# First batch in four groups per head pair, two 128-token first blocks, and a kept staging tile: a fused attention and two-layer feed-forward kernel

## The chip, the cores and the metric

The kernel runs on one core of a Trainium2 chip. TensorE (PE) multiplies matrices; VectorE (DVE), ScalarE (ACT) and GpSimd (POOL) do the elementwise work; SyncE (SP) issues most transfers. The metric is the device time of one execution in microseconds, as the median of three runs.

## What is computed

Thresholded attention over 4 batches of 8 heads, 576 positions and 64 features; its output, 2304 tokens of 512 features, goes through two feed-forward layers with 2048 hidden features each, all in 32-bit floats:

```python
scores = (q @ k.T) / sqrt(64)
thresh = max(scores) - tau
scores = where(scores >= thresh, scores, -1e9)
attn = exp(scores - max(scores)); attn /= sum(attn) + 1e-9
x = (attn @ v)                       # to [2304 tokens, 512]
h = x @ w_in;  g = where(h > 0, h, exp(min(h, 0)) - 1);  x = g @ w_out     # layer 0
h = x @ w2_in; g = maximum(0.01 * h, h);                 out = g @ w2_out  # layer 1
```

## The kernel before

**Attention.** Heads are worked in pairs, four pairs a batch. The 576 query rows of a batch are cut into nine units of 64 rows, and the units into groups (`GROUPS`): before, each batch has a group of four units and one of five. `group()` loads one tile `in` (keys and queries) and one tile `v` for each group and pair, and then takes the units two at a time: the score matmuls into `s` (L475), scale and row maximum on DVE (L479), threshold (L485), two passes on ACT (L490, L493), reciprocal (L496), and the scaling of `e` on POOL (L498). The probabilities must then be turned so that keys lie on partitions. There are two ways. In the first group of batch 0 (`gi < GP`) TensorE turns them: five 128x128 transposes for each unit into the accumulator tile `y` (L513), copied to `p` by ACT or DVE (L318, L319). In all other groups DVE turns blocks of 32x32 (L518) into `t`, and sixteen transfers move them to `p` (L568). `values()` multiplies `p` by `v` (L582), and a copy writes the result to `x`.

**Layer 0, first half of its hidden features**, is worked beside the attention in seven blocks of 256 tokens (`BESIDE`). A block has eight steps: `step_h` (four matmuls of 128 features each into `h`), the nonlinearity on ACT, POOL or DVE, and two steps later `step_y` into `y`. The first block (`NATIVE = 1`) multiplies plain 32-bit floats (L621, L674); the others split each operand into a high and a low part and make three passes (L624, L678). The tile `y` is one buffer of two banks, used in turn by all transposes of L513 and by the blocks, in the order in which the program names them. The `h` tile holds two steps, `gh` three. `evac_a` copies a block's `y` to the staging tile `ysa` and sends that to memory.

**The rest** follows when the attention is done: `close_attn` gives back its memory, and 512-token blocks run for what is left of layer 0 and for layer 1.

**The order.** Each engine's instructions are put in order ahead of time by a list scheduler in the program (`Order.run`): every operation carries a due time made from the numbers in `KN`, and a choice of engines. On the chip each engine then works strictly in that order, waiting where an operand is not there.

Of the kernel before, what the change touches and what calls it, by code (L numbers as in the profile page):

```python
# [10 lines left out]
F32 = mybir.dt.float32  # L11
# [19 lines left out]
GROUPS = [(b, u0, u1) for b in range(B) for u0, u1 in ((0, 4), (4, NU))]  # L31
UM = 5
WT = 32 * UM
BESIDE = 7
GP = 1
PT = ()
NG = 5
POOLI = 520
SPI = 720
# [4 lines left out]
NATIVE = 1  # L44
# [8 lines left out]
    pad=18, stay=1957.74, late=1.3, margin=0, look=0.00236881, warm=2, tu=2525.65, lead=19496.6, wv0=975.379,  # L53
    wv1=-2861.01, early=3673.33, boff=26347.2, bdt=5788.03, yoff=6965.78, coff=5895.83, wb=140.292, w2a=-207.297,
    b0=0, b1=0, b2=0, bd0=9322.68, vl=22862.5, tl=13509.4, wp0=137202, wp1=-2346.6, o1=-5700.07, o2=1859.51,
    o3=-792.8, o4=-3200.93, o5=4767.88, o6=-24.0285, mo=-2162.59, ka='P', kl='PA', kh='PA', ko='P', kt='D', kx='A',
    kxl='DP', km='DP', kg='A', kgl='DP', kgl1='D', kd='P', kc='AD', kn='P', kv='AD')
# [205 lines left out]
def attn_moe_kernel(ctx, tc, kqv, tau, w1i, w1o, w2i, w2o, yp, out):  # L263
# [20 lines left out]
    ysx = []  # L284
# [95 lines left out]
    ysx.append(ac.tile([128, KC, TA], F32, name="ysa"))  # L380
# [46 lines left out]
    def group(gi, p, vts, held=None):  # L427
# [24 lines left out]
        by_pe = gi < GP or p in PT  # L452
# [236 lines left out]
    ypdone = {}  # L689

    def block(layer, t0, fs, tb, deps, hps, yrings, evac, vt0, dt, reg=False):
        if reg and t0 < NATIVE * TA:
            xc = [(None, x[:, k, t0:t0 + tb], deps[k]) for k in range(KC)]
        else:
            xc = conv_x(t0, tb, deps, vt0 - dt + (KN["coff"] if reg else 0), reg)
        pend, lasty = [], None
        if isinstance(yrings, Ring):
            gen = yrings.new()
            ybank = [(gen, m % 2, m % 2 == 1) for m in range(KC)]

            def ysl(yg, m):
                return yg()[:, m // 2, m % 2 * TA:(m % 2 + 1) * TA]
# [12 lines left out]
        evac(t0, tb, ybank, ysl, lasty, xc, vt0 + len(fs) * dt)  # L715

    def evac_a(t0, tb, ybank, ysl, last, xc, vt):
        ys = ys_r.new()
        done = []
        if ybank[0][0] is ybank[1][0]:  # L720
            yg = ybank[0][0]
            for j in range(2):
                done.append(op(copy_of("AD", 2 * TA, lambda j=j: ys()[:, 2 * j:2 * j + 2, 0:TA],
                                       lambda j=j: yg()[:, j, :].rearrange("p (a b) -> p a b", a=2)),
# [37 lines left out]
    kept, ready = None, {}  # L762
    for gi, p in order:
# [7 lines left out]
        if gi < GP or p in PT or u == NP * NU:  # L771
# [16 lines left out]

    for i in range(BESIDE):
        need = next(n for t, n in ends if t >= (i + 1) * TA)  # L790
        block(0, i * TA, list(range(FH)), TA, x_deps(i * TA, TA), h_a, ya, evac_a,
              need * TU + KN["boff"] + (KN["b0"], KN["b1"], KN["b2"], 0)[min(i, 3)], KN["bd0"] if i == 0 else KN["bdt"],
              reg=True)
# [5 lines left out]
    end_a = op((HOST, 0, lambda: close_attn()), list(od.ops), [], 0)  # L799
# [16 lines left out]
    rest = [(t0, tb) for t0, tb in ((t, min(TB, NT - t)) for t in range(BESIDE * TA, NT, TB))]  # L816
# [76 lines left out]
```

## Time and profile before

| | |
|---|---|
| median of three runs | 1041.89 us (1040.13 to 1044.59) |
| profiled execution | 1044.41 us, its span 1042.6 us |
| PE busy | 1005.2 us, 96% |
| DVE, ACT, POOL busy | 569.2, 507.0, 392.0 us |
| chain that ended last | PE 90% of the span |

Busy time counts an instruction from its start to its end, and matmuls overlap, so work is better counted by the spacing of starts. An instruction's idle time is put down to what released it. The attention runs to about 400 us; after 402 us TensorE has hardly a gap.

### The profile page before, as it was taken

The page shows a single profiled execution, that of the slowest core. Times are in us where ns is not written, and L with a number is a line of the kernel's source. Part 1 is how long each engine was busy: PE and PEld are TensorE (multiplying, and loading weights), DVE is VectorE, ACT ScalarE, POOL GpSimd, SP SyncE. Part 2 cuts the span into 40 slices and gives each one's busy share as a digit, 9 for nine tenths or more (in the row PEclk, how much of TensorE's full clock was granted, in tenths as well). Part 3 has the DMA queues.
Part 4 walks back from the last instruction along what each step waited for, and adds up shares of the span by engine and source line. Part 5 has one row for each costly group of instructions (what it writes and reads, how often), then busy time and mean ns, then how long its engine had stood idle before and what let it go on. Part 6 is the DMA issues. An engine that isn't in the chain of part 4 may idle for free.

```text
span 1042.6 us, 17014 instructions
## 1 busy us (share of the span) xinstructions
PE 1005.2 (96%) x6228; PEld 795.3 (76%) x6228; DVE 569.2 (55%) x1146; ACT 507.0 (49%) x1009; POOL 392.0 (38%) x542
## 2 busy tenths in 40 slices
PE   6869999999999998999999999999999999999998
PEld 3446676677676776888888889888888888888898
DVE  6888778787887856767786457442211311311121
ACT  6967767677777753555455235432222311322221
POOL 5678977567577752444443013440000000000000
PEclk8999999999999999999999999999999999999999
DMA  6676876766778653353443103320100100000010
GB/s 213 209 216 175 221 195 192 227 188 196 201 209 240 192 150 119 102 182 101 143 141 101 61 21 86 118 61 0 41 1 1 41 1 1 22 19 1 1 41 21
DMA packets 47554, 115.93 MB, mean 111 GB/s; under 512 B 9776, under 2 KB 14384, under 8 KB 47472
## 3 DMA queue, kind: packets, MB, share of 16 engines
q1 hardware_dynamic: 42960, 104.36, 33.4%
q0 software_dynamic: 4512, 10.50, 3.7%
q8 instruction: 49, 0.80, 0.3%
q14 instruction: 33, 0.27, 0.1%
HBM read 67.63 MB, written 9.44 MB: 74 GB/s over the span
## 4 chain that ended last, share of the span: by engine, by line
PE 90%; DVE 3%; DMA 2%; ACT 2%; issue 1%; POOL 0%; SPq 0%; ACTq 0%; DVEq 0%; POOLq 0%
PE y L678 37%; PE h L624 22%; PE hb L624 15%; PE v L582 7%; PE s L475 7%; PE y L674 1%; DMA p<-t 1%; PE h L621 1%; DVE w L346 1%; DMA taut<-in_tau_dram 1%; DVE ss L479 1%; DMA wraw<-in_w1i_dram 1%; PE y L513 0%; DVE xl L307 0%; ACT e L493 0%
## 5 line engine op out<-in xcount | busy, mean ns | idle before, releaser
L307 DVE TENSOR_TENSOR gl<-g,gh 128x512 fp32r<-128x512 f32 (+1 forms) x150 | 101.1, 675 | 284.4 <-ACT g L656 265.0
L678 PE MATMUL y<-gh,woh 128*128 128x512 f32 (+1 forms) x704 | 245.5, 349 | 2.1 <-ACT ysa L318 1.4
L678 PE MATMUL y<-gl,woh 128*128 128x512 f32 (+1 forms) x704 | 242.8, 345 | 0.0
L624 PE MATMUL h<-xh,wih 128*128 128x256 f32 (+1 forms) x448 | 153.1, 342 | 9.2 <-ACT g L639 5.1
L678 PEld LDWEIGHTS y<-gh,woh 128*128 128x128 f32 x704 | 132.5, 188 | 29.1 <-issue 8.8
L624 PE MATMUL h<-xl,wih 128*128 128x256 f32 (+1 forms) x448 | 148.6, 332 | 0.7 <-DVE xl L307 0.6
L678 PEld LDWEIGHTS y<-gl,woh 128*128 128x128 f32 x704 | 132.7, 188 | 16.1
L498 POOL TENSOR_SCALAR e<-e,su 128x576 f32<-128x576 f32 x144 | 113.9, 801 | 32.2 <-DVE su L496 30.9
L678 PE MATMUL y<-gh,w 128*128 128x256 f32 (+1 forms) x384 | 124.9, 325 | 0.0
L490 ACT ACTIVATE ss<-ss,thr 128x576 f32<-128x576 f32 x144 | 104.6, 767 | 34.5 <-DVE thr L485 34.4
L479 DVE TENSOR_SCALAR_CACHE_REDUCE ss<-s,scl 128x576 f32<-128x576 f32 x144 | 113.8, 798 | 10.9 <-PE s L475 10.7
L678 PE MATMUL y<-gh,wol 128*128 128x512 f32 (+1 forms) x320 | 117.7, 368 | 0.0
L518 DVE STREAM_TRANSPOSE t<-e 128x640 f32<-128x640 f32 x128 | 101.2, 823 | 17.9 <-POOL e L498 12.5
L493 ACT ACTIVATE e<-ss,taun 128x577 f32<-128x577 f32 x144 | 110.5, 768 | 0.3
L624 PEld LDWEIGHTS h<-xh,wih 128*128 128x128 f32 x448 | 84.2, 188 | 33.2 <-issue 8.8
L475 PE MATMUL s<-in 64*64 64x288 f32 x1152 | 91.3, 428 | 7.8 <-DVE ss L479 7.8
L624 PE MATMUL hb<-xh,wih 128*128 128x512 f32 (+1 forms) x256 | 94.6, 369 | 0.0
L624 PE MATMUL hb<-xl,wih 128*128 128x512 f32 (+1 forms) x256 | 94.5, 369 | 0.0
L582 PE MATMUL v<-p,v 128*64 128x320 f32 (+1 forms) x640 | 87.1, 417 | 5.3 <-DVE p L319 2.3
L624 PEld LDWEIGHTS h<-xl,wih 128*128 128x128 f32 x448 | 84.3, 188 | 10.0 <-DVE xl L307 1.8
L624 PE MATMUL h<-xh,w 128*128 128x256 f32 (+1 forms) x288 | 89.3, 310 | 0.0
L654 ACT ACTIVATE gh<-h 128x512 fp32r<-128x512 f32 (+1 forms) x40 | 22.2, 555 | 132.4 <-PE h L624 132.4
(207 smaller groups left out, 1591.4 us busy)
## 6 DMA issues: line engine op xcount, KB each, us to landing
p<-t SPq DMA_DIRECT2D x128, 100.0 KB, 2.8
p<-t SPq DMA_DIRECT2D x144, 80.0 KB, 3.3
v<-in_kqv_dram SPq DMA_DIRECT2D x32, 320.0 KB, 3.8
in<-in_kqv_dram SPq DMA_DIRECT2D x16, 608.0 KB, 4.2
in<-in_kqv_dram SPq DMA_DIRECT2D x16, 544.0 KB, 4.0
wraw<-in_w1i_dram SPq DMA_DIRECT2D x16, 512.0 KB, 4.3
wraw<-in_w1o_dram SPq DMA_DIRECT2D x16, 512.0 KB, 3.6
wraw<-in_w2i_dram SPq DMA_DIRECT2D x16, 512.0 KB, 3.5
```

The costliest lines, as they stand in the source:

```text
L307: return pick(who, D=(dve(n), lambda: nc.vector.tensor_tensor(**args()), PORT), P=(pool_tt(n), lambda: nc.gpsimd.tensor_tensor(**args())))
L346: ob = op((DVE, dve(512), lambda: nc.vector.scalar_tensor_tensor(out=b().bitcast(U32), in0=top(), scalar=0x80000000, in1=b().bitcast(U32), ...
L475: nc.tensor.matmul(s[z]()[64 * h:64 * h + 64, i, 0:HALF], q()[r, at:at + 64], k()[r, h], start=True, stop=True)
L479: om = [op((DVE, dve(S) + 160, lambda z=z: nc.vector.tensor_scalar(out=ss[z]()[:, 0:S].rearrange("p (j c) -> p j c", j=2), in0=s[z]()[:, : ...
L490: o = op((ACT, act(S) + 95, lambda z=z: nc.scalar.activation(out=ss[z]()[:, 0:S], in_=ss[z]()[:, 0:S], func=AF.Prelu, bias=thr()[:, z:z + ...
L493: oe.append(op((ACT, act(S) + 190, lambda z=z: nc.scalar.activation(out=e[z]()[:, 0:S + 1], in_=ss[z]()[:, 0:S + 1], func=AF.Exp, bias=tau ...
L498: on = [op(pick(KN["kn"], P=(pool_ts(S) + 90, lambda z=z: nc.gpsimd.tensor_scalar(out=e[z]()[:, 0:S], in0=e[z]()[:, 0:S], scalar1=su()[:, ...
L518: turned.append(op((DVE, dve(SX) + 70, lambda z=z, cols=cols: nc.vector.transpose(out=blocks(tg).rearrange("p d c q -> p c d q")[:, :, :, ...
L582: nc.tensor.matmul(ps()[64 * h:64 * h + 64, 0:64 * n], v()[:, h, c, :], blocks(pg)[:, 2 * h:2 * h + 2, c], start=(c == 0), stop=(c == 4))
L624: nc.tensor.matmul(hp(), w_()[:, cs], x_()[:, 0:tb], start=(k == 0 and z == 0), stop=(k == KC - 1 and z == 2))
L654: o1 = op((ACT, actp(tb), lambda: nc.scalar.activation(out=gh()[:, cs], in_=hp(), func=AF.Prelu, alpha=0.01)), [o], [hg, gh], vt)
L678: nc.tensor.matmul(ysl(yg, m), w_()[:, cs], g_()[:, 0:tb], start=(first and z == 0 and share == 0), stop=(last and z == 2 and end))
```

## The change

Batch 0 is cut into four groups of 2, 2, 2 and 3 units for each pair (`CUTS`); the first three are turned by TensorE (`GP = 3`). The other batches keep their two groups. The first block of 256 tokens becomes two of 128 (`HEADS`), both in plain 32-bit floats (`NATIVE = 2`); six blocks of 256 tokens follow as before. The staging tile `ysa` moves from the attention's memory to memory that is kept, and the operation that closes the attention's memory depends on what was named before the last block's copies out of `y`, not on those copies and their transfer. The numbers in `KN` differ, with the engines allowed to some operations among them (for example the copies from `v` to `x`: DVE alone; the subtraction `gl` beside the attention: POOL alone).

```diff
-GROUPS = [(b, u0, u1) for b in range(B) for u0, u1 in ((0, 4), (4, NU))]
+CUTS = (2,4,6)
+GROUPS = [(b, u0, u1) for b in range(B) for u0, u1 in zip((0, *(CUTS if b == 0 else (4,))), (*(CUTS if b == 0 else (4,)), NU))]
+HEADS = [(0, 128), (128, 128)]
+FIRST = HEADS + [(t, TA) for t in range(256, 1792, TA)]
-BESIDE = 7
-GP = 1
+GP = 3
-NATIVE = 1
+NATIVE = 2
...
-    ysx = []
+    ysx = [const.tile([128, KC, TA], F32, name="ysa")]
...
-    ysx.append(ac.tile([128, KC, TA], F32, name="ysa"))
...
     def evac_a(t0, tb, ybank, ysl, last, xc, vt):
+        since[0] = len(od.ops)
...
-    for i in range(BESIDE):
-        need = next(n for t, n in ends if t >= (i + 1) * TA)
+    for i, (t0, tb) in enumerate(FIRST):
+        need = next(n for t, n in ends if t >= t0 + tb)
...
-    end_a = op((HOST, 0, lambda: close_attn()), list(od.ops), [], 0)
+    end_a = op((HOST, 0, lambda: close_attn()), od.ops[:since[0]], [], 0)
```

How the order moves is seen at three places. First, TensorE near the start. Names: `s` scores, `y<-ident` a turned unit, `v<-p` the values of a group, `h<-x` the first block. Before:

```order
L475 MATMUL s<-in 64x288 x8
L582 MATMUL v<-p_86,v 64x256 x10
L513 MATMUL y<-ident,e_90 128x128 x5
L475 MATMUL s<-in 64x288 x8
L513 MATMUL y<-ident,e_91 128x128 x5
L621 MATMUL h<-x,w_143 128x256
```

And with the change:

```order
L477 MATMUL s<-in 64x288 x8
L515 MATMUL y<-ident,e_93 128x128 x5
L584 MATMUL v<-p_87,v 64x128 x10
L515 MATMUL y<-ident,e_90 128x128 x5
L477 MATMUL s<-in 64x288 x8
L515 MATMUL y<-ident,e_91 128x128 x5
L623 MATMUL h<-x,w_143 128x128
L584 MATMUL v<-p_86,v 64x128 x10
```

The values of a group now come after every second turned unit, not every fourth, and are half as wide.

Second, TensorE where the first block's `y` begins. Before, it stands behind the sixteenth turned unit and some steps of `h`:

```order
L513 MATMUL y<-ident,e_93 128x128 x5
L582 MATMUL v<-p_87,v 64x256 x10
L621 MATMUL h<-x,w_143 128x256
L621 MATMUL h<-x,w_230 128x256
L475 MATMUL s<-in 64x288 x8
L621 MATMUL h<-x,w_230 128x256 x3
L475 MATMUL s<-in 64x288 x12
L621 MATMUL h<-x,w_324 128x256 x4
L674 MATMUL y<-gh,w_196 128x256 x4
L621 MATMUL h<-x,w_439 128x256 x2
L582 MATMUL v<-p_86,v 64x320 x10
```

With the change:

```order
L477 MATMUL s<-in 64x288 x8
L515 MATMUL y<-ident,e_93 128x128 x5
L584 MATMUL v<-p_87,v 64x128 x10
L676 MATMUL y<-gh,w_178 128x128 x2
L477 MATMUL s<-in 64x288 x4
L676 MATMUL y<-gh,w_178 128x128 x2
L676 MATMUL y<-gh,w_282 128x128 x4
L676 MATMUL y<-gh,w_384 128x128 x4
L477 MATMUL s<-in 64x288 x8
L623 MATMUL h<-x,w_704 128x128 x4
```

It stands behind the twenty-fourth turned unit and the twelfth group's values, with five steps of `h` already ahead of it.

Third, the end of the attention. On DVE, `xh` and `xl` are the split input of the first 512-token block. Before:

```order
L319 COPY ysa<-y 128x512 x2
L319 COPY x<-v 128x2x5x32
L307 TENSOR_TENSOR xl_5030<-x,xh_5011 128x512
L307 TENSOR_TENSOR xl_5034<-x,xh_5028 128x512
```

With the change:

```order
L322 COPY ysa<-y 128x512
L322 COPY x<-v 128x2x5x32
L317 TENSOR_SCALAR xh_5297<-x 128x512
L317 TENSOR_SCALAR xh_5312<-x 128x512
L310 TENSOR_TENSOR xl_5316<-x,xh_5293 128x512
```

Two of the four high parts now stand on DVE (before, all four on ACT). On TensorE the last group's values are followed by six matmuls of the last 256-token block, which before stood ahead of them.

## Rows read from the trace of the kernel before

**Rows 1.** Stretches of 25 us: busy (instructions) by engine, granted clock, DMA share, GB/s.

```profile
25.00:50.00 25.00, 20.98 (x184) 12.48 (x184) 20.28 (x48) 23.18 (x45) 17.42 (x22) 0.93 0.64 201
50.00:75.00 25.00, 17.64 (x124) 10.29 (x116) 22.88 (x47) 19.55 (x40) 17.82 (x25) 0.93 0.74 221
...
425.00:450.00 25.00, 25.00 (x112) 20.68 (x112) 20.29 (x27) 14.53 (x24) 11.41 (x10) 1.00 0.29 90
```

**Rows 2.** TensorE in order of time: start, length, instruction, [idle before <-releaser].

```profile
14.78 1.18 PE L513 MATMUL y<-ident,e 128*128 128x128 f32 x5 [0.57 <-POOL e L498]
...
37.58 0.77 PE L513 MATMUL y<-ident,e 128*128 128x128 f32 x5
38.28 1.20 PE L475 MATMUL s<-in 64*64 64x288 f32 x16
39.41 0.77 PE L513 MATMUL y<-ident,e 128*128 128x128 f32 x5
...
44.44 2.38 PE L582 MATMUL v<-p,v 128*64 128x256 f32 x20 [0.78 <-ACT p L318]
46.75 0.77 PE L513 MATMUL y<-ident,e 128*128 128x128 f32 x5
...
52.27 0.74 PE L513 MATMUL y<-ident,e 128*128 128x128 f32 x5
54.38 2.38 PE L582 MATMUL v<-p,v 128*64 128x256 f32 x20 [1.38 <-DVE p L319]
...
76.56 4.93 PE L582 MATMUL v<-p,v 128*64 128x320 f32 x20 [2.20 <-DMA p<-t]
81.42 1.20 PE L475 MATMUL s<-in 64*64 64x288 f32 x16
...
86.09 1.89 PE L621 MATMUL h<-x,w 128*128 128x256 f32 x8
87.82 0.59 PE L674 MATMUL y<-gh,w 128*128 128x256 f32 x2
...
92.10 2.91 PE L582 MATMUL v<-p,v 128*64 128x320 f32 x20
...
100.47 1.89 PE L621 MATMUL h<-x,w 128*128 128x256 f32 x8
```

**Rows 3.** One longer stretch, columns as in rows 1.

```profile
100.00:350.00 250.00, 243.49 (x2184) 176.26 (x2184) 198.04 (x494) 184.13 (x409) 182.12 (x294) 1.00 0.74 207
```

**Rows 4.** ACT and DVE groups by shape: count, then busy us and mean ns.

```profile
L338 ACT ACTIVATE w<-wraw,lowb 128x512 uint32<-128x512 uint32 x60 | 45.7, 761 | 27.7 <-POOL wil L308 8.8 <-POOL w L308 8.3 <-POOL wol L308 6.5
...
L346 DVE SCALAR_TENSOR_TENSOR w<-wraw,w 128x512 uint32<-128x512 uint32 x64 | 48.0, 750 | 1.2
...
L647 DVE SCALAR_TENSOR_TENSOR g<-g,h 128x512 f32<-128x512 f32 x20 | 13.7, 686 | 0.6
L647 DVE SCALAR_TENSOR_TENSOR gh<-g,h 128x256 f32<-128x256 f32 x8 | 3.3, 413 | 0.8 <-ACT g L639 0.7
```

**Rows 5.** Transfers from 0 to 75 us: packets and bytes; issues, KB each, us to landing.

```profile
DMA packets 4875, 16.07 MB, mean 214 GB/s; under 512 B 736, under 2 KB 736, under 8 KB 4869
in<-in_kqv_dram SPq DMA_DIRECT2D x4, 608.0 KB, 4.0
...
v<-in_kqv_dram SPq DMA_DIRECT2D x6, 320.0 KB, 3.6
```

**Rows 6.** The end of the attention in order of time, TensorE, DVE and ACT.

```profile
395.94 0.39 PE L678 MATMUL y<-gh,woh 128*128 128x256 f32 x1 [0.78 <-DVE ysa L319]
396.50 3.12 PE L582 MATMUL v<-p,v 128*64 128x320 f32 x20
...
399.66 0.49 DVE L319 COPY x<-v 128x320 f32<-128x320 f32 x1 [2.36 <-PE v L582]
401.39 2.20 ACT L313 ACTIVATE xh<-x 128x512 fp32r<-128x512 f32 x4 [9.63 <-DMA yp_dram<-ysa]
402.07 0.50 PE L624 MATMUL h<-xh,wih 128*128 128x512 f32 x1 [2.46 <-ACT xh L313]
```

More of the change, by code (lines that the diff above doesn't have):

```diff
@@ L30 @@
 NU = S // 64
-GROUPS = [(b, u0, u1) for b in range(B) for u0, u1 in ((0, 4), (4, NU))]
+CUTS = (2,4,6)
+GROUPS = [(b, u0, u1) for b in range(B) for u0, u1 in zip((0, *(CUTS if b == 0 else (4,))), (*(CUTS if b == 0 else (4,)), NU))]
+HEADS = [(0, 128), (128, 128)]
+FIRST = HEADS + [(t, TA) for t in range(256, 1792, TA)]
 UM = 5
 WT = 32 * UM
-BESIDE = 7
-GP = 1
-PT = ()
+GP = 3
+PT = set()
 NG = 5
+LP = 0
 POOLI = 520
-SPI = 720
+SPI = 700
 PM = ()
@@ L52 @@
 KN = dict(
[L53 to L57, printed above, removed]
+    pad=18, stay=8085.79, late=1.3, margin=0, look=0.00236881, warm=2, tu=2269.97, lead=19258.9, wv0=5061.38,
+    wv1=-3081.32, early=3673.33, boff=26347.2, bdt=5825.03, yoff=8020.93, coff=5895.83, wb=406.105, w2a=-207.297,
+    b0=0, b1=0, b2=0, bd0=11622.3, vl=20762.4, tl=16711.4, wp0=185209, wp1=-2003.44, o1=-5700.07, o2=1859.51,
+    o3=-57.8519, o4=1496.36, o5=3550.58, o6=-24.0285, mo=-2162.59, ka='P', kl='A', kh='PA', ko='P', kt='D', kx='AD',
+    kxl='DP', km='DP', kg='A', kgl='P', kgl1='DP', kd='P', kc='AD', kn='P', kv='D')
 PE, ACT, DVE, POOL, SP, HOST = "PE", "ACT", "DVE", "POOL", "SP", "HOST"
@@ L689, in attn_moe_kernel, with block @@
     ypdone = {}
-    def block(layer, t0, fs, tb, deps, hps, yrings, evac, vt0, dt, reg=False):
-        if reg and t0 < NATIVE * TA:
+    since = [0]
+    def block(layer, t0, fs, tb, deps, hps, yrings, evac, vt0, dt, reg=False, whole=False):
+        if whole:
             xc = [(None, x[:, k, t0:t0 + tb], deps[k]) for k in range(KC)]
@@ L762, in attn_moe_kernel @@
     kept, ready = None, {}
+    PT.update(order[len(order) - LP:])
     for gi, p in order:
@@ L787, in x_deps @@
                  if b * S + 64 * u0 < t0 + tb and b * S + 64 * u1 > t0] for k in range(KC)]
-    for i in range(BESIDE):
-        need = next(n for t, n in ends if t >= (i + 1) * TA)
-        block(0, i * TA, list(range(FH)), TA, x_deps(i * TA, TA), h_a, ya, evac_a,
-              need * TU + KN["boff"] + (KN["b0"], KN["b1"], KN["b2"], 0)[min(i, 3)], KN["bd0"] if i == 0 else KN["bdt"],
-              reg=True)
+    for i, (t0, tb) in enumerate(FIRST):
+        need = next(n for t, n in ends if t >= t0 + tb)
+        block(0, t0, list(range(FH)), tb, x_deps(t0, tb), h_a, ya, evac_a,
+              need * TU + KN["boff"] + (KN["b0"], KN["b1"], KN["b2"], 0)[min(i, 3)],
+              KN["bd0"] if i < NATIVE else KN["bdt"], reg=True, whole=i < NATIVE)
         if i == NATIVE - 1:
@@ L814, in dt @@
         return 24 * mm(tb)
-    rest = [(t0, tb) for t0, tb in ((t, min(TB, NT - t)) for t in range(BESIDE * TA, NT, TB))]
+    rest = [(t0, tb) for t0, tb in ((t, min(TB, NT - t)) for t in range(sum(FIRST[-1]), NT, TB))]
     ysb = {}
```

10 lines of the change are left out of this document (5 added, 5 removed).

## The prediction

> **What bounds the kernel now.** I read the stretches of 25 us first. From 425 us on TensorE is busy all 25 of 25 us, and from 100 to 350 us 243.5 of 250 [rows 1, 3]; before that it is not: 21.0 of 25 from 25 to 50 us and 17.6 from 50 to 75 us, at a granted clock of 0.93 [rows 1]. So the end is set by TensorE's work plus the time it loses in the first 80 us or so and at the close of the attention. Who holds it up early is read from the busy shares there: from 25 to 50 us ACT is busy 23.2 of 25 us and DVE 20.3, and from 50 to 75 us DVE 22.9 [rows 1]. TensorE is fed at the pace of these two. The order of time then shows single stalls: 1.38 us before the values at 54.38, which wait for a copy of a turned unit, and 2.20 us before those at 76.56, which wait for the transfers of the turned blocks and then take 4.93 us where the same take 2.91 at 92.10 [rows 2]. The other place is the close of the attention: 0.78 us for a copy out of `y`, and 2.46 us before the first 512-wide matmul, because ACT's split of its input waits for the transfer of the staging tile [rows 6].
>
> **The measure.** TensorE works strictly in its order, so I compare two moments: when the changed kernel has as much TensorE work left as the kernel before has at 81.42 us, where its long stalls end. Durations are spacings of starts [rows 2]: two units of scores 1.13 us (38.28 to 39.41), so 0.565 a unit; one turned unit 0.70 (37.58 to 38.28); values of four units 2.31 (44.44 to 46.75, length 2.38), of five, with the same overlap, 2.91 - 0.07 = 2.84; a native 256-wide matmul 1.73 / 4 = 0.43 (86.09 to 87.82).
>
> Before, ahead of 81.42 us stand, by the program's order, 28 units of scores (15.8), 16 turned units (11.2), four values of four units and one of five (9.2 + 2.8), 14 matmuls of `h` and 4 of `y` (7.8): 46.9 us of work. The warm-up is the same in both and left out.
>
> **Groups of 2, 2, 2 and 3, turned by TensorE.** *Added work.* Eight more units are turned: 8 x 0.70 = 5.6 us. Values of two and three units are not in the trace; one step of 64 columns is worth 2.84 - 2.31 = 0.53, so I take 1.25 and 1.78 us. Above, if a turned unit's 0.70 for five passes of 128 columns (0.14 each, two side by side in the 20 passes) is the nearest, it is 1.4; the far end is no gain over the four units' 2.31, below it is half of that, 1.16. With 1.25, a pair costs 3 x 1.25 + 1.78 - 2.31 - 2.84 = 0.4, and four pairs 1.5 us (range +0.4 to +3.5, far end +14). The four groups of batch 0 that DVE turns keep their sixteen transfers each, smaller ones. Eight more loads of `in` and `v` go on SP's queue; with them and all weights, 12 x 0.426 + 4 x 0.492 + 16 x 0.328 + 16 x 0.524 = 20.7 MB are asked for before TensorE's first `y`, against 16.07 MB in the first 75 us before [rows 5]. Loads of 320 KB land in 3.6 us and of 608 KB in 4.0 [rows 5], so the first load, 416 KB where it was 544, saves 0.2 us at most, and I leave it out.
>
> The Trainium skill, "DMA: Bandwidth & Descriptors", section "Anatomy of one DMA", gives a transfer a fixed part of about 2.0 us that size does not change; the two loads agree with a large fixed part. If instead a load went by its bytes alone, 416 KB would land some 0.9 us sooner than 544 and the forecast would be that much lower.
>
> *What it moves.* All transposes and all block accumulations share the one tile `y`, in program order. So the first `y` of the block now waits for the twenty-fourth turned unit, not the sixteenth, although its `h` could start sooner; three `gh` and two `h` let only five steps of `h` (20 matmuls, 4.4 us) run ahead. Before the first `y`, then: 32 units of scores (18.1), 24 turned (16.8), twelve values (15.0), 20 half-width matmuls (4.4): 54.3 us of work.
>
> *When that is.* Before, the first turned unit stands at 14.78 and the sixteenth at 52.27: 2.50 us a unit [rows 2]. With the change the same stretch holds 16 weights in 24 units against 9 in 16; a tenth of a weight more a unit, at 0.76 us on ACT and two operations of 0.75 on DVE [rows 4], is 0.08 to 0.15 us, and twelve small copies to `x` in place of four add about 0.04. The chain on TensorE gives the same. Copy and hops after a turned unit's 0.7 take about 1.4, as the 2.1 us from the turned unit at 52.27 to the values at 54.38 show [rows 2]; so turned unit and copy 2.1, values 1.25, next turned unit and copy 2.1 with the scores beside it, 5.4 for two units. I take 2.7. The twenty-fourth turned unit then starts at 14.78 + 23 x 2.7 = 76.9; from a last turned unit to its values it is 54.38 - 52.27 = 2.1, and the values take 1.25: first `y` at 80.3 us, 1.1 earlier than 81.42.
>
> **Two first blocks of 128 tokens.** 128 matmuls of half width for 64: at half of 0.43 and a little (0.222), 28.4 for 27.7 us, +0.7. If two passes of 128 columns cost 2 x 0.14 each as in a turned unit, +8.1; below, +0. I keep near the half, as the 256-wide ones go by columns. The work left at the first `y` is thus 5.6 + 1.5 + 0.7 - (54.3 - 46.9) = 0.4 us more than before at 81.42. Behind it each step of 128 tokens offers TensorE 1.8 us while its nonlinearity passes ACT, POOL and DVE, all 71 to 92% busy from 50 to 75 us [rows 1]; I allow 2.5 us of waits in the next 20 us against 1.05 before (81.42 to 100.47 holds 18.0 us of work): +1.5 (0 to 5).
>
> On DVE the step of 256 columns takes 413 ns and that of 512 takes 686 [rows 4]; the line through them leaves 140 ns that width does not change, so sixteen narrow ones cost 16 x 0.277 - 8 x 0.413 = 1.1 us more on DVE, beside other work. The Trainium skill, "VectorE: DVE Perf Modes", section "The TRN2 errata", says the same against this part of the change, that small operations pay a fixed latency each and should be widened; the two rows agree. With cost by columns alone the 1.1 would be 0.
>
> **The staging tile kept.** The split of the input no longer waits for the transfer, but in DVE's order it stands behind the copy of the last values. From the end of those values (396.50 + 3.12 = 399.62): copy 0.5, two high parts and one low part about 1.8, a hop, so the second matmul about 2.55 us later; 0.75 of that is now filled by the six matmuls moved behind the values. Some 1.7 us of idle time remain of 0.78 + 2.46, and the next matmul's short wait goes with it: -1.8 (0 to -3.5). If the split still waits for something of the last block, it is 0.
>
> **The numbers in the table** send subtractions to POOL and copies to DVE. From 100 us on TensorE hides these; its gaps up to 350 us were 6.5 us [rows 3], and I leave it at 0, with 3 us either way.
>
> **Sum:** -1.1 + 0.4 + 1.5 - 1.8 = -1.0. Against the profiled execution's 1044.4 us (span 1042.6) that is 1043.4; it lay 2.5 above the median of 1041.89, so **1040.9** in terms of the median. A measurement of this kernel can tell some 0.5%, 5.2 us, from no change.
>
> **Rivals.** *The early stretch runs better than I charge.* In the order DVE copies nine of the 24 turned units (ACT fifteen) and has turned only three itself by the first `y`, so it is freed of part of its load while it is the fuller engine; all weights are asked for before the first transfers of turned blocks, which came 2.2 us late at 76.56 [rows 2] with weights between them in SP's queue. With 2.50 us a unit and no extra waits the first `y` is at 75.6: -4.7 - 1.5 more, -7.2, **1034.7**. Against it speaks ACT, busy 23.2 of 25 us [rows 1], which copies more than before.
>
> *The turning loop becomes the bound, and the kernel is slower.* On TensorE's queue the values of a group now stand after every second unit and wait for the copy of the unit just turned; behind them stand the next turned unit and the scores, so ACT and DVE are fed late too. Before, the waits there were 0.78 and 1.38 us for four units [rows 2]. One such wait for two units is 0.2 to 0.35 us a unit more, and if ACT and DVE, fed late, do not make it up, a unit takes 3.1 us: first `y` at 89.4, +9.1, **1050**. It decides from about 2.97 us a unit, where +6.2 on the forecast makes the kernel over 0.5% slower.
>
> *Transfers become the bound.* At the mean rate of before, 214 GB/s, 20.7 MB take 97 us: +16, **1057**; it decides below 240 GB/s. Against it, the engines of DMA were busy only 0.74 of the time at 221 GB/s [rows 1], which leaves room to about 300.
>
> *The staging tile does nothing* (the memory is still held by the last values): +1.8, **1042.7**.
>
> **How the numbers follow.** The forecast, with the staging rival, holds 0.45, all of it within 0.5% (its own range 1037 to 1045); the better early stretch 0.35, faster; the turning loop 0.15 and the transfers 0.05, slower. So faster 0.35, same 0.45, slower 0.20. The range goes from 1032, a little under the first rival for the waits of the middle (0 to -3), to 1049, below the loop's 1050, and leaves out less than 2 in 10.
>
> **What would show it.** In the profile of the changed kernel: the first `y` of the native block near 80 us; turned units 2.7 us apart, with what ends the idle time before the values of two units; values of two units near 1.25 us; half-width matmuls near 0.22; the gap before the first 512-wide matmul under 2 us, ended by DVE's low part and no longer by a transfer; more than 240 GB/s in the first 75 us. The prediction is wrong if the first `y` comes before 76 or after 86 us, or if TensorE's gaps from 100 to 395 us change by more than 3 us.

## The result and the profile after

The changed kernel takes **1058.85 us** (median of 4 runs, 1056.17 to 1061.53) where the kernel before took 1043.24 on the same chip (4 runs, 1040.13 to 1044.79): ratio 1.0133, 95% interval 1.0096 to 1.0170. By the ratio it is slower by some 14 us (the two medians differ by 15.6); 1040.9 had been forecast, with a range from 1032 to 1049. Its profiled execution took 1058.3 us (span 1056.5), the one before 1044.4 (span 1042.6), so the two traces differ by the same 13.9 us.

A good place to cut both traces is the first 512-wide matmul, where the attention has closed: 402.07 us before [rows 6], 414.72 after. Behind it TensorE is busy nearly all the time and the two kernels need 640.5 and 641.8 us, so 12.65 of the 13.9 us are lost ahead of it and 1.25 behind it. TensorE alone, in stretches (bounds, length, busy and instructions, granted clock, DMA share, GB/s), first the kernel before, then the changed one:

```profile
0.00:402.07 402.07, 368.98 (x3156) 0.98 0.70 200
0.00:100.00 100.00, 78.92 (x586) 0.91 0.65 203
100.00:402.07 302.07, 290.06 (x2571) 1.00 0.71 199
```

```profile
0.00:414.72 414.72, 380.39 (x3485) 0.98 0.69 199
0.00:100.00 100.00, 79.52 (x774) 0.90 0.69 223
100.00:414.72 314.72, 300.88 (x2715) 1.00 0.69 191
```

Busy time rose by 11.4 us (368.98 to 380.39), and idle time, length less busy, did not fall: 33.1 before, 34.3 after. The forecast had 7.8 us of added work (5.6 + 1.5 + 0.7) and an end 1.0 us earlier, so it needed the idle time to shrink by 8.8, to 24.3. In the first 100 us TensorE does 79 us of work in both kernels; the added work is not done there in the gaps, it pushes other work behind 100 us, where busy time grew by 10.8.

The stretches of rows 1 and 3 in the changed kernel (busy and instructions of TensorE, its weight loads, DVE, ACT and POOL, then granted clock, DMA share, GB/s):

```profile
25.00:50.00 25.00, 19.00 (x209) 13.67 (x198) 18.69 (x47) 19.30 (x37) 12.70 (x18) 0.93 0.76 260
50.00:75.00 25.00, 22.51 (x258) 16.14 (x254) 21.68 (x55) 22.47 (x47) 13.30 (x20) 1.00 0.81 257
...
100.00:350.00 250.00, 239.44 (x2190) 177.74 (x2186) 196.72 (x480) 169.92 (x379) 190.18 (x299) 1.00 0.70 196
```

From 50 to 75 us TensorE is fuller than before (22.5 for 17.6), from 25 to 50 us emptier, and from 100 to 350 us it idles 10.6 us in place of 6.5. TensorE in order of time, as rows 2. First, two of the earliest scores in the kernel before:

```profile
9.20 2.20 PE L475 MATMUL s<-in 64*64 64x288 f32 x16 [2.68 <-DVE ss L479]
12.01 2.20 PE L475 MATMUL s<-in 64*64 64x288 f32 x16 [0.61 <-DVE ss L479]
```

Then the changed kernel:

```profile
9.48 2.20 PE L477 MATMUL s<-in 64*64 64x288 f32 x16 [2.90 <-DMA in<-in_kqv_dram]
12.58 2.20 PE L477 MATMUL s<-in 64*64 64x288 f32 x16 [0.91 <-DMA in<-in_kqv_dram]
16.04 1.33 PE L515 MATMUL y<-ident,e 128*128 128x128 f32 x5 [1.26 <-POOL e L500]
...
34.47 0.76 PE L515 MATMUL y<-ident,e 128*128 128x128 f32 x5
...
39.53 2.30 PE L584 MATMUL v<-p,v 128*64 128x128 f32 x20 [1.30 <-DVE p L322]
41.76 1.33 PE L515 MATMUL y<-ident,e 128*128 128x128 f32 x5
...
64.72 0.77 PE L515 MATMUL y<-ident,e 128*128 128x128 f32 x5
65.41 1.20 PE L477 MATMUL s<-in 64*64 64x288 f32 x16
66.61 0.74 PE L515 MATMUL y<-ident,e 128*128 128x128 f32 x5
68.12 1.31 PE L584 MATMUL v<-p,v 128*64 128x128 f32 x20 [0.78 <-ACT p L321]
69.37 0.77 PE L515 MATMUL y<-ident,e 128*128 128x128 f32 x5
...
81.64 0.77 PE L515 MATMUL y<-ident,e 128*128 128x128 f32 x5
84.05 1.31 PE L584 MATMUL v<-p,v 128*64 128x128 f32 x20 [1.64 <-ACT p L321]
85.29 0.71 PE L676 MATMUL y<-gh,w 128*128 128x128 f32 x4
...
86.58 2.50 PE L676 MATMUL y<-gh,w 128*128 128x128 f32 x20
89.01 1.20 PE L477 MATMUL s<-in 64*64 64x288 f32 x16
...
95.77 0.71 PE L623 MATMUL h<-x,w 128*128 128x128 f32 x4 [1.15 <-DVE gh L649]
```

The turned units stand at 16.04 (first) and 81.64 (twenty-fourth), 2.85 us a unit; the first `y` of the native block at 85.29 (70.99 in the kernel before; the 81.42 us that the prediction measures from is a later moment). A pair of units without other matmuls between can be read from 64.72 to 69.37: turned unit 0.69, scores 1.20, turned unit 0.73, 0.78 of waiting for its copy, values 1.25, together 4.65 us. Other pairs take longer, by matmuls of `h`, by longer waits, and by the clock: the pair from 34.47 to 41.76 takes 7.29, with values that wait 1.30 us and then take 2.23 in place of 1.25. What TensorE waited for from 14 to 85 us (us in all, times, the longest):

```profile
PE v L584 <- ACT p L321: 6.5, 6, 1.6
PE y L515 <- DVE p L322: 2.3, 3, 1.0
PE v L584 <- DVE p L322: 2.2, 2, 1.3
```

These are waits for copies of turned units, 11.0 us of the 13.6 that TensorE idles there; none of its waits there is for a transfer.

The close of the attention, as rows 6, TensorE and then DVE and ACT:

```profile
410.14 2.91 PE L584 MATMUL v<-p,v 128*64 128x320 f32 x20
...
414.72 0.50 PE L626 MATMUL h<-xh,wih 128*128 128x512 f32 x1 [0.77 <-ACT xh L316]
```

```profile
413.10 0.49 DVE L322 COPY x<-v 128x320 f32<-128x320 f32 x1 [2.16 <-PE v L584]
414.04 0.76 DVE L317 TENSOR_SCALAR xh<-x 128x512 fp32r<-128x512 f32 x2 [0.45 <-PE y L680]
414.03 1.16 ACT L316 ACTIVATE xh<-x 128x512 fp32r<-128x512 f32 x2 [6.86 <-PE y L680]
```

TensorE idles 0.77 us before its first 512-wide matmul where 0.78 + 2.46 stood around the last values [rows 6]. ACT's split starts 0.44 us after DVE's copy of the last values, and what released it was no transfer. Transfers from 0 to 75 us, as rows 5:

```profile
DMA packets 5865, 17.91 MB, mean 239 GB/s; under 512 B 672, under 2 KB 672, under 8 KB 5857
```

### The profile page after: what moved, and what is told of

Its sections match the earlier page's. It is cut to its first block, busy times and chain, and to the rows that moved or that the text cites. A ratio compares the mean times of both kernels' runs of the same rounds, so it can differ in the third digit from the quotient of the medians.

```text
span 1056.5 us, 17766 instructions
## 1 busy us (share of the span) xinstructions
PE 1017.1 (96%) x6556; PEld 814.8 (77%) x6556; DVE 581.0 (55%) x1187; ACT 491.3 (47%) x979; POOL 405.7 (38%) x565
## 4 chain that ended last, share of the span: by engine, by line
PE 82%; DVE 6%; DMA 3%; issue 3%; POOL 3%; ACT 2%; SPq 1%; DVEq 0%; POOLq 0%; ACTq 0%
PE y L680 33%; PE h L626 20%; PE hb L626 14%; PE v L584 6%; PE s L477 5%; PE h L623 1%; PE y L676 1%; DMA p<-t 1%; DVE t L520 1%; DVE ss L481 1%; PE y L515 1%; DVE xl L310 1%; DMA in<-in_kqv_dram 1%; DVE w L349 1%; DMA taut<-in_tau_dram 1%
## 5 line engine op out<-in xcount | busy, mean ns | idle before, releaser
L310 DVE TENSOR_TENSOR gl<-g,gh 128x512 fp32r<-128x512 f32 (+1 forms) x122 | 91.3, 748 | 278.2 <-ACT g L658 260.1
L311 POOL TENSOR_TENSOR gl<-g,gh 128x256 fp32r<-128x256 f32 (+1 forms) x54 | 42.4, 788 | 315.9 <-ACT g L658 207.8
L492 ACT ACTIVATE ss<-ss,thr 128x576 f32<-128x576 f32 x144 | 104.6, 767 | 35.3 <-DVE thr L487 34.8
L500 POOL TENSOR_SCALAR e<-e,su 128x576 f32<-128x576 f32 x144 | 107.7, 758 | 20.9 <-DVE su L498 19.0
L520 DVE STREAM_TRANSPOSE t<-e 128x640 f32<-128x640 f32 x120 | 95.2, 825 | 15.2 <-POOL e L500 8.5
L584 PE MATMUL v<-p,v 128*64 128x128 f32 (+3 forms) x800 | 90.0, 372 | 10.6 <-ACT p L321 6.5
```

The costliest lines, as they stand in the source:

```text
L310: return pick(who, D=(dve(n), lambda: nc.vector.tensor_tensor(**args()), PORT), P=(pool_tt(n), lambda: nc.gpsimd.tensor_tensor(**args())))
L311: P=(pool_tt(n), lambda: nc.gpsimd.tensor_tensor(**args())))
L492: o = op((ACT, act(S) + 95, lambda z=z: nc.scalar.activation(out=ss[z]()[:, 0:S], in_=ss[z]()[:, 0:S], func=AF.Prelu, bias=thr()[:, z:z + ...
L500: on = [op(pick(KN["kn"], P=(pool_ts(S) + 90, lambda z=z: nc.gpsimd.tensor_scalar(out=e[z]()[:, 0:S], in0=e[z]()[:, 0:S], scalar1=su()[:, ...
L520: turned.append(op((DVE, dve(SX) + 70, lambda z=z, cols=cols: nc.vector.transpose(out=blocks(tg).rearrange("p d c q -> p c d q")[:, :, :, ...
L584: nc.tensor.matmul(ps()[64 * h:64 * h + 64, 0:64 * n], v()[:, h, c, :], blocks(pg)[:, 2 * h:2 * h + 2, c], start=(c == 0), stop=(c == 4))
```

## The experiments

Theory: the parts of the change add up, and the added work of the groups lies in idle time. Rivals: the table holds the loss; the groups or the narrow blocks cost by themselves. All ratios are against the kernel before, run beside each. The last four columns are read from the profiled execution up to the first 512-wide matmul: its start, TensorE's busy and idle time, and the time that TensorE spent at 1.2 GHz (summed up to 430 us over stretches of 5 us, each counted as length x (1 - granted clock) / 0.5). These columns are of one execution each, and that can lie off the median: by 3.9 us below it in 13 and 3.5 in 14. The last one differs between executions of the same kernel: over the 71 executions of the kernel before that stand beside these runs the granted clock of the whole span went from 0.984 to 0.993, by the same count 34 to 15 us at 1.2 GHz, some 22 in the mean; the profiled one is at 0.992. The changed kernel's four runs are at 0.990 and 0.991, some 21 us, so its loss is not one of the clock.

| kernel | ratio (95%) | start | busy | idle | 1.2 GHz |
|---|---|---|---|---|---|
| before | 1 | 402.1 | 369.0 | 33.1 | 17.1 |
| changed | 1.0133 (1.0096-1.0170) | 414.7 | 380.4 | 34.3 | 20.4 |
| 1 before, staging kept | 0.9986 (0.9968-1.0004) | 401.3 | 369.7 | 31.6 | 17.0 |
| 2 before, changed table | 1.0165 (1.0146-1.0185) | 416.4 | 377.0 | 39.5 | 34.2 |
| 3 changed, groups of before | 1.0144 (1.0120-1.0168) | 416.4 | 375.1 | 41.4 | 20.5 |
| 4 changed, one first block | 1.0127 (1.0101-1.0153) | 413.7 | 378.8 | 34.8 | 13.6 |
| 5 changed, table of before | 1.0091 (1.0059-1.0123) | 412.1 | 380.3 | 31.8 | 17.0 |
| 6 before, groups and staging | 1.0135 (1.0103-1.0168) | 418.8 | 379.8 | 38.9 | 20.5 |
| 7 before, narrow blocks and staging | 1.0101 (1.0064-1.0138) | 412.3 | 375.7 | 36.6 | 27.4 |
| 8 before, table: engines only | 1.0134 (1.0094-1.0174) | 414.4 | 375.1 | 39.3 | 23.8 |
| 9 before, table: numbers only | 1.0109 (1.0065-1.0153) | 411.5 | 373.0 | 38.5 | 20.4 |
| 10 before, `kx` alone | 1.0074 (1.0049-1.0098) | 409.0 | 373.2 | 35.8 | 20.4 |
| 11 before, `tu` + 1% | 0.9977 (0.9955-1.0000) | 399.3 | 369.8 | 29.5 | 17.2 |
| 12 changed, `kx` of before | 1.0107 (1.0076-1.0137) | 411.3 | 377.6 | 33.7 | 13.7 |
| 13 before, longer turned units | 1.0022 (1.0000-1.0045) | 402.5 | 372.2 | 30.3 | 13.7 |
| 14 before, matmuls halved | 1.0013 (0.9989-1.0036) | 400.6 | 370.1 | 30.5 | 17.2 |
| 15 changed, longer turned units | 1.0167 (1.0134-1.0199) | 417.7 | 386.4 | 31.4 | 13.7 |
| 16 changed, less work on ACT | 1.0112 (1.0085-1.0140) | | | | |
| 17 changed, less work on DVE | 1.0122 (1.0097-1.0147) | 415.3 | 381.5 | 33.8 | 20.5 |
| 18 before, staging and `tu` + 1% | 0.9968 (0.9950-0.9986) | 398.0 | 368.7 | 29.4 | 13.7 |

### One part at a time (1 to 7)

```
1, in before:  ysx = [const.tile([128, KC, TA], F32, name="ysa")]
               close_attn() waits for od.ops[:since[0]], not for list(od.ops)
2, in before:  KN = the changed kernel's table
```

> The kernel before with one part of the change: the staging tile kept and the close of the attention no longer behind the last block's copies. Theory (TensorE pays for added work and for the late start, and the staging part gains): TensorE's gaps at the close fall from 0.78 + 2.46 + 0.22 us to about 1.0, the first 512-wide matmul at about 399.7 to 400.5 instead of 402.07, time 1.5 to 2.5 us under before. Rival (the loss sits in the close or in what follows it): no gain or a loss here, and gaps after the close.

> The kernel before with the changed table of numbers alone. Theory (the structure costs, not the table): within 4 us of before. Rival (the table, which hands subtractions to POOL and copies to DVE, makes waits between 100 and 400 us): 5 to 10 us slower than before, with TensorE's gaps from 100 to 350 us well above the 6.5 us of before.

The staging tile alone gives some 1.5 us, which the interval cannot tell from nothing; the trace shows the gap before the first 512-wide matmul at 0.72 us, ended by ACT's split, where 2.46 stood [rows 6], but that matmul came at 401.3 us and not at 399.7 to 400.5. The table alone costs 17 us, where "within 4 us" had been expected: that theory fell. Its 14.4 us ahead of the first 512-wide matmul are 6.4 us of idle time and 8.0 us of busy time with the same matmuls. In this execution the second is mostly the clock: 17 us more at 1.2 GHz, of which some 14 ahead of the close, worth at most 7 us at half speed. Over all runs that share is smaller: the four of kernel 2 are at 0.982 to 0.987, 33 us at 1.2 GHz in the mean, 11 more than the kernel before, worth at most 5.5 of the 17 us. And kernel 9 has 4.0 us more busy time with no more time at 1.2 GHz ahead of its close (3.4 of its 20.4 us lie behind it), so not all such busy time is the clock. The pattern can be read in one place of kernel 2:

```profile
129.21 0.39 PE L624 MATMUL h<-xh,wih 128*128 128x256 f32 x1 [1.58 <-DVE xh L314]
131.93 0.58 PE L624 MATMUL h<-xl,wih 128*128 128x256 f32 x1 [2.33 <-POOL xl L308]
...
134.78 4.10 PE L582 MATMUL v<-p,v 128*64 128x256 f32 x20
```

```profile
130.00:135.00 5.00, 2.60 (x10) 0.65 0.65 172
135.00:140.00 5.00, 5.00 (x37) 0.67 0.94 271
100.00:350.00 250.00, 237.67 (x2089) 0.99 0.71 201
```

Two waits, 3.9 us together, for the halves of an input split that the table now sends to DVE and POOL; behind them, at a granted clock of 0.67, the values of four units take 4.10 us where they take 2.38 [rows 2]. The last line is the longer stretch of rows 3, with gaps of 12.3 us for 6.5.

```
3, in changed:  CUTS = (4,)   GP = 1
4, in changed:  HEADS = [(0, 256)]   NATIVE = 1
5, in changed:  KN = the table of before
6, in before's table:  groups of the change, one first block of 256, staging kept
7, in before's table:  groups of before, two first blocks of 128, staging kept
```

> The changed kernel with batch 0 cut and turned as before (groups of 4 and 5, the first turned by TensorE); half-width first blocks, staging and table stay as changed. Theory (the turned units and narrow values add 7 us of TensorE work, and the turning loop at 2.85 us a unit starts the block late): first y near 70 us, 9 to 13 us faster than the changed kernel, near the kernel before. Rival (table or half-width blocks hold the loss): within 4 us of the changed kernel.

> The changed kernel with one first block of 256 tokens in place of two of 128. Theory (a half-width native matmul takes 0.245 us, not half of 0.43, so the two blocks cost 31.4 - 27.7 = 3.7 us): 2 to 5 us faster than the changed kernel, first y still behind the twenty-fourth turned unit near 85 us. Rival (half-width blocks are what fills the early gaps, as they can begin sooner): slower than the changed kernel by 2 us or more.

> The changed kernel with its groups, its two first blocks of 128 tokens and its kept staging tile, but with the table of numbers of the kernel before. Measured so far: the changed table alone in the kernel before gives 1061 us, 17 more than before, while the whole change gives 14 more. Theory (the parts add up): the three other parts are worth -2 to -3 us, so this kernel takes 1040 to 1044 us, and the first 512-wide matmul stands near 400 us. Rival (the table was right for the groups, and the groups cost by themselves): turning eight more units, smaller values and half-width matmuls put some 11 us of work on TensorE before 415 us, and this kernel takes 1052 us or more.

> The kernel before with the groups of 2, 2, 2 and 3 units (three turned by TensorE) and the kept staging tile, one first block of 256 tokens, the table of before. Theory (parts add up): near the table-of-before kernel of the same call, less the 1.5 us that the two narrow blocks cost, so 1039 to 1043 us. Rival (the groups cost by themselves): the 8.6 us of added turning and values show, 1050 us or more. If this is fast and the table-of-before kernel slow, the two narrow blocks are to blame; both slow, the groups.

> The kernel before with the two first blocks of 128 tokens and the kept staging tile; groups and table as before. Theory (parts add up): the narrow blocks cost 1.6 to 2 us of work on TensorE and staging gives 2.4 back, so 1042 to 1045 us. Rival (a new order loses as such): 1050 us or more, by idle time and not by work.

Taking one part out of the change (3, 4, 5) gains nothing that can be told apart; 9 to 13 and 2 to 5 us had been expected of 3 and 4. Putting one part into the kernel before (2; 6 and 7 with the staging tile) costs 10 to 17 us each time. Together they cost 14: the parts do not add, and the theory that they do fell in 5, 6 and 7. One rival is not tested by this: numbers of a table may suit only the groups that they came with. Kernel 2 runs the changed table with the old groups, 5 to 7 the old table with new groups or blocks, and no run set the numbers anew, so each of these losses may hold a misfit.

Kernel 5 shows best what the groups and blocks do, because its table and its time at 1.2 GHz are those of before:

```profile
0.00:412.06 412.06, 380.25 (x3484) 0.98 0.68 200
0.00:100.00 100.00, 78.45 (x769) 0.91 0.66 217
100.00:412.06 312.06, 301.79 (x2716) 1.00 0.69 195
100.00:350.00 250.00, 243.21 (x2215) 1.00 0.71 202
```

All of its 10 us are busy time, 11.3 us more than before, and idle time is 1.3 less, no more than the staging tile gives. By the spacing of starts 5.1 us of the 11.3 are turned units, 3.4 values and 2.1 the native blocks. Every kernel with the groups has 377.6 us of work or more ahead of the close, and none, 15 with its longer units aside (31.4), has less than 31.8 us of idle time beside it.

In 7, which has no groups, the loss comes otherwise: ahead of the close 3.5 us of it are idle time and 6.7 busy time, and of the latter 10.3 us more at 1.2 GHz are worth at most 5.1. Its place with the longest wait, and the values behind it at the lower clock:

```profile
137.85 0.43 PE L626 MATMUL h<-xh,wih 128*128 128x256 f32 x1 [3.61 <-ACT g L641]
...
139.28 3.44 PE L584 MATMUL v<-p,v 128*64 128x256 f32 x20
```

```profile
135.00:145.00 10.00, 6.65 (x47) 0.83 0.61 154
```

### Which entries of the table (8 to 12)

```
8, in before:   kl='A' kx='AD' kgl='P' kgl1='DP' kv='D'
9, in before:   all numbers of the changed table, letters of before
10, in before:  kx='AD'
11, in before:  tu=2550.91
12, in changed: kx='A'
```

> The kernel before with only the table's choices of engine of the changed kernel: the low part of the weights on ACT alone (POOL or ACT before), the high part of the input on ACT or DVE (ACT before), the low part of the gate on POOL alone (DVE or POOL before) during the attention and on DVE or POOL behind it, copies of the values on DVE alone (ACT or DVE before). Theory (the choices take away the planner's second engine): most of the 17 us, 1054 us or more. Rival (the due times hold the loss): within 4 us of before, 1040 to 1048.

> The kernel before with only the table's numbers of the changed kernel (due times of weights, units, blocks, transfers and the bonus for staying with the same kind of matmul), the choices of engine as before. Theory (the choices of engine hold the loss): within 4 us of before, 1040 to 1048. Rival (the due times hold it): 1054 us or more, with the first 512-wide matmul after 410 us.

> The kernel before with one of the five choices of engine alone: the high part of the input on ACT or DVE, where it was on ACT. No work is added; a quarter of TensorE's matmuls stand elsewhere. Theory (this choice is one of those that hold the loss of the choices, 14 us): 1050 us or more. Rival of single causes (it is another choice): within 4 us of before. Rival of the new order (any one loses): 1050 us or more too, so together with the unit-time run: both slow speaks for the new order as such, one alone for a single cause.

> The kernel before with one number of the table, tu (the due time from one unit to the next), raised by 1%: no work is added, but about a quarter of TensorE's matmuls and a third of DVE's and a half of ACT's instructions stand elsewhere in the order. Theory (single entries of the changed table cost, each for a reason of its own): within 4 us of before, 1040 to 1048. Rival (any new order of the units loses what this order happened to fit, some 9 to 14 us): 1052 us or more, with 5 us more idle time before the first 512-wide matmul.

> The changed kernel with one entry of its table as before: the high part of the input on ACT alone. In the kernel before the opposite change cost 8 us. Theory (that entry costs by itself, DVE takes splits for which it has no room): 4 us or more faster than the changed kernel, 1050 to 1055 us. Rival (what an entry costs depends on the order it falls into): within 4 us of the changed kernel's 1059, or slower.

Letters and numbers cost 14 and 11 us each, 17 together. So I asked whether every new order loses: not this one. With `tu` 1% higher at least a sixth of TensorE's matmuls stand elsewhere, by their names in the two traces, and the kernel is no slower (11). One letter, `kx`, costs 8 us alone (10). Set back in the changed kernel it moved the ratio from 1.0133 to 1.0107 with overlapping intervals (12), so a gain of its own there is not shown.

### The work itself (13 to 15)

```
13, 15:  for c in range(5): turn(...)   ->   for c in (0, 1, 2, 3, 4, 0, 1, 2): turn(...)
14, in before: each native matmul as two of 128 columns, same place in the order
```

> The kernel before, in the same order on all engines; each of its 16 turned units makes three of its five transposes twice (8 in place of 5), so TensorE gets 16 x 3 x 0.14 = 6.7 us more work before 55 us, about what the eight more turned units of the change give it. Theory A (the idle time of TensorE there is a chain turned unit, copy, values, next turned unit, in which added work stands in line): 5 to 7 us slower than before, 1049 to 1051 us, idle time before the first 512-wide matmul about 33 us as before. Rival B (the 19.5 us of idle time ahead of 75 us take it in, as the prediction counted): at most 2 us slower, idle time about 27 us.

> The changed kernel in its own order; each of the 24 turned units makes three of its five transposes twice, 24 x 3 x 0.14 = 10.1 us more work on TensorE before 82 us. Theory (with values behind every second unit the turned unit stands in a chain that nothing covers, so its length adds): 6 us or more slower than the changed kernel, 1064 us and more, a turned unit every 3.1 us or more. Rival (idle time takes it in, as in the kernel before, where 6.7 us added cost about 2): at most 4 us slower, 1058 to 1063, a turned unit every 2.85 to 3.0 us.

> The kernel before, in the same order on all engines: each of the 128 native 256-wide matmuls of its first block is made as two of 128 columns, and nothing else is narrowed (one block, one chain of 256 columns on the other engines). Two of half width at 0.245 us, as the changed kernel shows them, against 0.43 put 64 x 2 x (2 x 0.245 - 0.43) = 7.7 us more into the places of the 128, or by the prediction's 0.222 only 1.8. Theory (the narrow blocks cost by TensorE's work): 4 us or more slower than before, 1048 us and more. Rival (they cost by the narrower chain of steps and the new order around it): at most 2 us slower, 1043 to 1047.

In 13 the added work is 5.3 us (16 units, 0.33 each). In the profiled execution, the fastest of ten, idle time falls by 2.8 us and busy time rises by 3.3, with 3.4 us less at 1.2 GHz that are worth at most 1.7; over all ten the kernel is 2.3 us slower (0 to 4.7). Longer turned units in an unchanged order are thus about half hidden, between A and B and nearer to B. In 15, from the first to the last turned unit,

```profile
15.82 1.97 PE L515 MATMUL y<-ident,e 128*128 128x128 f32 x8 [1.14 <-POOL e L500]
...
85.00 1.09 PE L515 MATMUL y<-ident,e 128*128 128x128 f32 x8
...
88.64 0.71 PE L676 MATMUL y<-gh,w 128*128 128x128 f32 x4
```

it is 3.01 us a unit for 2.85, with each unit 0.33 longer, and the kernel is some 3.5 us slower (1.0167 against 1.0133, with overlapping intervals) for 8 us of work. Idle time falls by 3.0 us there; 6.7 us less at 1.2 GHz, worth at most 3.4, hide as much again, so 15 says less than 13. In 14 the expectation counted 128 native matmuls; there are 64, so at 0.245 it should have said 3.8 us. It is 1.4 us slower (-1.1 to 3.8). Eight halves in a row take 1.79 us, 0.224 each:

```profile
83.11 1.95 PE L622 MATMUL h<-x,w 128*128 128x128 f32 x16
84.90 0.61 PE L677 MATMUL y<-gh,w 128*128 128x128 f32 x4
```

(a count of 16 is eight matmuls, each in two passes). So neither the length of a turned unit (13) nor the width of a matmul (14) holds the loss by itself.

### What sets the pace ahead of the first `y` (16, 17)

```
16, in changed:  out=ss[z]()[:, 0:64 if gi < GP else S]   (ACT's thresholding step)
17, in changed:  out=b().bitcast(U32)[:, 0:64 if reg else 512]   (DVE's second step on a weight)
```

What the two leave out: 16 thresholds 64 of the 576 columns of the turned units, and 17 sets the signs of 64 of the 512 columns of the first sixteen weights.

> The changed kernel in its own order, with one piece of ACT's work left out: for the 24 units that TensorE turns, the thresholding step on ACT works on 64 of its 576 columns (the rest stays as it was, so the attention of these units is not the reference's). By the trace the step takes 0.77 us at 576 columns and 0.27 at 128, so some 24 x 0.5 = 12 us of ACT's time ahead of 82 us are gone. Theory (ACT's pace feeds TensorE in the turning stretch, and TensorE's work there is moved behind 100 us for that reason): a turned unit every 2.5 us or less, first y at 77 us or earlier, 6 us or more faster than the changed kernel, 1053 us or less. Rival (the chain turned unit, copy, values, next turned unit sets the pace): a turned unit still every 2.75 us or more, within 3 us of the changed kernel.

> The changed kernel in its own order, with one piece of DVE's work left out: the second of DVE's two steps on each of the first 16 weights works on 64 of its 512 columns (the signs of the rest are lost, so the first layer is not the reference's). By the trace a step takes 0.71 us at 512 columns and 0.28 at 128, so some 16 x 0.45 = 7 us of DVE's time ahead of 82 us are gone. Theory (DVE's pace feeds TensorE there): a turned unit every 2.6 us or less, first y 5 us or more earlier, 4 us or more faster than the changed kernel, 1055 us or less. Rival (ACT, or the chain through TensorE, sets the pace): first y within 2 us, within 3 us of the changed kernel.

The stretch of the turned units, columns as rows 1, in the changed kernel, in 16 and in 17:

```profile
14.00:85.00 71.00, 57.41 (x614) 39.90 (x608) 57.60 (x142) 61.11 (x120) 38.03 (x55) 0.92 0.70 230
```

```profile
14.00:85.00 71.00, 58.29 (x620) 40.63 (x612) 58.73 (x144) 53.23 (x120) 38.49 (x56) 0.91 0.69 230
```

```profile
14.00:85.00 71.00, 58.93 (x641) 41.52 (x634) 53.89 (x152) 63.70 (x126) 39.48 (x61) 0.94 0.70 233
```

ACT loses 7.9 us of 61.1 in the first; the first `y` comes at 84.41 in place of 85.29 and a turned unit every 2.82 us, so that theory fell. DVE loses 3.7 of 57.6 in the second; the first `y` comes at 82.19, 3.1 us earlier, between the 5 of the theory and the 2 of its rival. Of these 3.1 us, 0.8 stand already at the first turned unit (15.22 for 16.04), and the granted clock of 0.94 for 0.92 is worth some 1.5 (the changed kernel's 1.2 GHz around 40 us is missing in 17), so DVE's part in the pace (2.75 us a unit) is small if there is one. Neither kernel's time differs from the changed one's by more than the intervals. (The profiled execution of 16 took 9 us more than its median, so only its first 85 us are used.) By elimination the pace is that of TensorE's own row of turned unit, scores, copy and values, which it works off strictly in order; the 11.0 of 13.6 us spent waiting for copies of turned units fit that, but no run shortened that row, so this is argued and not shown. Nor did the earlier first `y` of 17 bring an earlier end: in the same execution the first 512-wide matmul stood at 415.3 for 414.7.

### A better version (18)

```
18, in before:  tu=2550.91, staging kept as in 1
```

> The kernel before with the kept staging tile and the unit time raised by 1%, the two that were each some 2 us better than before. If both gains add up (one at the close of the attention, one ahead of it): 1039 to 1041 us, ratio near 0.996. If they are the same gain (the close of the attention is better in both): about 1042.

1041.40 us against 1044.78: 0.3% faster than the kernel before (0.1 to 0.5), and so faster than both. The gains of 1 and 11, 1.5 and 2.4 us, neither of them clear of noise by itself, come close to adding up (3.3 us), and the idle time is the lowest of all, by 0.1 us.

## Why the prediction was wrong, point by point

From -1.0 to +13.9 the sum missed by 14.9 us: 5.0 at the first `y`, 5.0 in the work left, 3.7 in the idle time between the first `y` and the close (-0.3 forecast, waits and staging tile together, and +3.4 measured) and 1.25 behind the close. By its own steps:

- **The first `y`** was to come at 80.3 us and came at 85.29, 3.9 later than 81.42 and not 1.1 earlier: **5.0 us**. The first turned unit stood at 16.04 and not 14.78 (+1.26), where the sum had left the start as it was: TensorE waited 2.90 and 0.91 us for loads at the two places where it had waited 2.68 and 0.61 for DVE, and then 1.26 us in place of 0.57 for POOL's `e`. The pace was 2.85 and not 2.7 (23 x 0.15 = +3.5). From the last turned unit through its values it was 3.65 and not 3.35. The prediction's chain for two units, 5.4 us, was too long for a bare pair (4.65) and too short for those with matmuls of `h`, more waits or the lower clock in them (up to 7.29). "TensorE is fed at the pace of these two" was not borne out: with 7.9 us less on ACT the first `y` moved by 0.9 us (16), and DVE's part is small if there is one (17).
- **The work left** was to be 0.4 us more and was 5.4 more: **5.0 us**. By the first `y` TensorE had done 66.33 us, against 60.34 before by 81.42: 6.0 more, not 7.4. And 11.4 us were added, not 7.8. Two prices were right: a turned unit 0.69 to 0.73 us (0.70 forecast), values of two units 1.25 (1.25). The third holds only inside a run: 0.222 was forecast for a half-width matmul and the eight of kernel 14 take 0.224 each, but in the changed kernel the run of ten from 86.58 to 89.01 takes 0.243 each, the two from 85.29 to 85.93 0.32, and all 128 of them 0.264 in the mean. By the spacing of starts, summed over all matmuls ahead of the close, the turned units added 5.5 us (5.6), the values 2.3 (1.5) and the native blocks 1.7 (0.7). The rest, some 1.9 us, is on scores and on `h` and `y` of the later blocks, which the change does not touch, and the sum had no term for it. The 3.3 us more at 1.2 GHz in this pair of traces are worth at most 1.6 of it all. Busy time also grows with the number of waits, 44 ahead of the close for 34, because the last matmul before each counts with its whole length, 0.28 us for 256 columns where the next one starts 0.12 behind it in a run: by estimate 1.6 us.
- **Waits behind it and the table**: idle time from the first `y` to the first 512-wide matmul is 15.4 us (329.43 less 314.06) against 12.0 (320.65 less 308.64). With the 2.5 us of the staging tile put back that is 5.8 more; 1.5 had been allowed for waits and **"I leave it at 0, with 3 us either way"** for the numbers in the table. That bound is the step that failed most clearly: "From 100 us on TensorE hides these" is refuted by kernel 2, 17 us slower with the table alone, and by gaps of 10.6 us for 6.5 from 100 to 350 us. In that stretch kernel 2 has gaps of 12.3 us and kernel 5, with the old table, 6.8; but 6 and 7, also with the old table, have 12.7 and 11.7, so the table is not the only source of such gaps. How much of the 14 us is the table's inside the whole change is less sure: 1.0133 against 1.0091 without it, some 4 us with overlapping intervals.
- **The staging tile** did as said: some 2.5 us by the trace (1.8 forecast), 1.5 by kernel 1. The step of 128 columns on DVE takes 288 ns (277 forecast). The Trainium skill, "VectorE: DVE Perf Modes", section "The TRN2 errata", says that small operations pay a fixed latency; the trace agrees, with 288 ns at 128 columns and 413 at 256 [rows 4].
- **Rivals.** *The turning loop* was the nearest: it named the pace, and decides from 2.97 us a unit. The pace stayed below that and the kernel was slower all the same, because the work left grew too. *Transfers* were to decide below 240 GB/s; the rate was 239, but the engines of DMA were no busier than 0.81 in the stretches shown, and TensorE's waits for loads add up to 3.8 us, all of them before the first turned unit. *The better early stretch* is refuted (85.29 for 75.6), and so is *the staging tile does nothing*.

The root of it: the forecast set the added work against idle time that it took for free room, and kernel 5 shows 11.3 us of added work with idle time only 1.3 lower. Why the room was not free is argued, not shown: it is part of a chain. Work put inside an unchanged chain was about half hidden (13), but more links of the chain (24 turned units and twelve short values ahead of the first `y` in place of 16 and five) take their own copies and waits along.

What stays open: why the narrow blocks or the groups alone cost as much as both together with the table (7, 6 and the changed kernel), which entry beside `kx` holds the rest of the table's 17 us, and how much of each loss is a table that does not suit its groups.

## What to carry to other kernels

Idle time of the bounding engine is room for more work only where nothing in it waits for that work; before counting on it, write the chain out link by link and add a link's copy and hops, not only its matmuls. A table of due times and engine choices is a part of the change like any other: price it by taking it alone, since here that cost 17 us, and by taking it out of the whole, where it was worth some 4 with overlapping intervals. Where the rows behind a wait on TensorE show the lower clock, count their extra length to the wait. And read time at 1.2 GHz from all runs of a kernel before it is called a cause, since it differs from one execution to the next.

## What was not expected of the hardware

Waits of 1.5 to 3.6 us in the middle of a busy stretch (129 to 132 us in kernel 2, 137.85 in kernel 7) were followed by work at 1.2 GHz: four units' values in 4.10 and 3.44 us for 2.38. Not every wait was: at its close, from 399 to 403 us, the kernel before was busy for 1.32 of 4 us, and the granted clock stayed at 1.00 there and in the 4 us behind. Up to 430 us the profiled execution of kernel 2 spent 34.2 us at 1.2 GHz and that of the kernel before 17.1. TensorE was busy for 25.8 and 15.5 us of such time ahead of the close, so this accounts for about 5 of the 8 us by which the same matmuls took longer. How much time a kernel spends there is not fixed by its program: over 71 executions of the kernel before the granted clock went from 0.984 to 0.993 and the time from 1040.5 to 1051.4 us.
